# Half swaps, a broadcast and 64-bit weight loads moved to other steps of an attention loop

## The chip, the cores and the metric

One core of a Trainium2 chip runs the whole program in one launch. The metric is the device time of one execution in microseconds (us). The kernel before took 1222.17 us (median of three runs, 1221.45 to 1222.9).

## What is computed

The reference chains three parts; the change lies in the first and touches how weights of the second arrive.

```python
# attention over 16 (batch, head) pairs, seq 1152, head_dim 64; queries are averaged in pairs: 576 per head
q_pool = q.reshape(B, H, S // 2, 2, D).mean(axis=3)
attn   = softmax(q_pool @ k.T / sqrt(D))
x      = (attn @ v)  ->  (1152, 512)
# a dense layer with mish: w_in is 512 x 2048, w_out is 2048 x 512, both 64-bit floats in memory
x = mish(x @ w_in) @ w_out
# eight experts, weighted by a gate that is normalised eight times over rows and columns
out = sum_e P[:, e] * (relu(x @ w1[e]) @ w2[e])
```

## The kernel before

TensorE works on a 32-bit format that keeps fewer bits than float32 (`F32R`), so each operand is split into a high and a low part ("hi" and "lo"), and a product is the sum of two or three matmuls.

**Attention in steps.** Two heads make a pair, and there are 8 pairs. A pair has 1152 pooled queries, nine tiles of 128 (`QTL` = 9): tiles 0 to 3 belong to the first head, 5 to 8 to the second, tile 4 (`MID`) holds 64 queries of each. One step of the loop at L715 handles one tile: step `g` is pair `p` and tile `t` by `divmod(g, 9)`; the document writes t0 to t8 for the step within a pair. There are 72 steps, then three that drain. In step g the engines' instructions are put out in this order:

- what was left in the list `first` by the step before (L722 to L725);
- `scores(g)` (L468): 6 matmuls (12 at t4) into `psS`, and on VectorE the negated row maximum into `e`;
- `prep` (L691): on GpSimd (POOL), splits of the next pair's q, k and v. The last of each splitting operation also starts the next load on POOL's queue (`load_kv` L343, `load_q` L350);
- the first entry of `pre`, the list made by `turn` (L699): transposes of k (`trans_k` L405) or q (`trans_q` L452);
- `transposes(g - 3)` (L546): nine transposes of the exponentials `er` into `psT`, evacuated by ScalarE (`eth`) and VectorE (`etl`);
- `hand_over(g - 1)` (L499): one DMA on the queue of SyncE (SP) copies the exponentials of the step before from `e` to `er`, 576 KB. `er` has two buffers, so this DMA waits until `transposes(g - 3)` have read theirs; `transposes(g - 1)` in step g + 2 need it landed;
- up to 9 matmuls of attention times values (`psA`), the rest of `pre`, and `exps(g)` on ScalarE;
- at t1, `turn_sums` (L510): a transpose of the row sums, a copy to `rt`. It leaves `out` in `first`; `out` (L519, at t2) sends the sums to a row in DRAM and leaves `back`; `back` (L523, at t3) reads them back broadcast over partitions into `rx` with three DMAs. `rx` is used by `split_x` (L603) on POOL after the pair's last `psA`;
- at last `run_all` (L114), which gives out what the queues "pool", "act", "dve" and "dma" hold for this step.

**Swaps.** A transposed q tile holds [hi; lo] over the 128 partitions, and its second copy has to hold [lo; hi]. `swap` (L447) makes that copy by two DMAs on SP's queue, of 64 partitions each. `trans_q(p, u)` transposes tiles 0 to 3 (u = 0), 5 to 8 (u = 1) or tile 4 (u = 2, into `qz`), and leaves its swap in `first`. The table `TURN` (L640) puts u = 0 at t6 of the pair before, u = 2 at t0 and u = 1 at t1. At t6 `turn` lists `trans_k(p + 1, 0, 1)` first and `trans_q(p + 1, 0)` second, so the second one follows after the step's `psA` matmuls. Pair 0 takes its queries another way, without swaps.

**64-bit weights.** `load_w` plans the conversion of 64-bit weights to F32R parts: `plan64` (L136) gives a DMA of 512 KB into `raw` (three buffers, L101), then shifts, sign and sum on POOL, VectorE and ScalarE, each with a due step. Six such blocks (`busy=True`, L625 and L626) are converted during attention, with first due steps 16, 25, 34, 43, 52 and 60, and `stage` = 2, so that L178 makes their DMAs due at 11.2, 20.2, 29.2, 38.2, 47.2 and 55.2: they go out at the end of steps 12, 21, 30, 39 and 48 (all t3) and 56 (t2).

So the order of SP's queue within a pair is: t1 the swap of `qz`, `hand_over`; t2 the swap of u = 1, `out`, `hand_over`; t3 `back`, `hand_over`, the weight load; t4 to t6 `hand_over`; t7 the swap of u = 0, `hand_over`; t8 and t0 `hand_over`. SP takes them strictly in this order, as do the other engines with theirs.

```python
            waiting = first + loads          # L722
            first[:], loads[:] = [], []
            for f in waiting:
                f()
            at(ts[0] - 2.4 * stage, "dma", dma)      # L178
            first.append(lambda: swap(t))            # L464
                first.append(back)                   # L521
```

Of the kernel before, what the change touches and what calls it, by code (L numbers as in the profile page):

```python
# [23 lines left out]
def pool_attention_mish_sinkhorn_kernel(  # L24
# [22 lines left out]
    NPAIR = B * H // 2  # L47
# [56 lines left out]
    def at(t, eng, f):  # L104
        queue[eng].append((t, f))
# [12 lines left out]
    def load_w(which, i, times, stage, late="pool", parts=1, busy=False):  # L118
# [11 lines left out]
        def hi(heng, c, x):  # L130
            split_hi(heng, dest()[0][:, c, :], x)

        def lo(c, x):
            split_lo(nc.vector if late == "dve" else nc.gpsimd, dest()[1][:, c, :], x, dest()[0][:, c, :])

        def plan64(u, t):  # L136
            box = {}

            def dma():
                raw = wraw.tile([P, 2 * GF], F32, tag="raw", name=f"raw{which}_{i}_{u}")  # L140
                nc.sync.dma_start(out=raw.bitcast(I64), in_=src[:, u, :])
                w = raw.rearrange("p (n two) -> p n two", two=2)
                box["l"], box["h"] = w[:, :, 0], w[:, :, 1]

            def scale(x):
                if x and busy:
                    nc.gpsimd.tensor_scalar(box["h"], box["h"], 2.0 ** -112, 0.0, op0=ALU.mult, op1=ALU.add)
                elif x:  # L150
                    nc.scalar.activation(box["h"], box["h"], AF.Copy, scale=2.0 ** -112)
                else:
                    nc.scalar.activation(box["l"].bitcast(I32), box["l"].bitcast(U32), AF.Copy, scale=2.0 ** -29)

            def shift(cs=slice(0, GF)):
                if "t" not in box:
                    box["t"] = wpools["t"].tile([P, GF], U32, tag="wt", name=f"wt{which}_{i}_{u}")
                h = box["h"][:, cs].bitcast(U32)
                if busy:
                    nc.vector.scalar_tensor_tensor(  # L160
                        out=box["t"][:, cs], in0=h, scalar=3, in1=mask.to_broadcast(list(h.shape)),
                        op0=ALU.logical_shift_left, op1=ALU.bitwise_and)
                else:
                    nc.vector.tensor_scalar(
                        box["t"][:, cs], h, 3, 0x7FFFFFF8, op0=ALU.logical_shift_left, op1=ALU.bitwise_and)

            def sign(cs=slice(0, GF)):
                t = box["t"][:, cs]
                nc.vector.scalar_tensor_tensor(  # L169
                    out=t, in0=box["h"][:, cs].bitcast(U32), scalar=0x80000000, in1=t,  # L170
                    op0=ALU.bitwise_and, op1=ALU.bitwise_or)

            def join():
                t = box["t"].bitcast(I32)
                nc.gpsimd.tensor_tensor(out=t, in0=t, in1=box["l"].bitcast(I32), op=ALU.add)  # L175

            ts = t if isinstance(t, tuple) else [t + j * stage for j in range(5)]
            at(ts[0] - 2.4 * stage, "dma", dma)  # L178
            at(ts[0], "pool" if busy else "act", lambda: scale(1))
            at(ts[0] + parts - 1, "act", lambda: scale(0))  # L180
            for j in range(parts):
                cs = slice(j * GF // parts, (j + 1) * GF // parts)
                at(ts[1] + 2 * j, "dve", lambda cs=cs: shift(cs))
                at(ts[1] + 2 * j + parts - 1, "dve", lambda cs=cs: sign(cs))
            at(ts[2], "pool", join)
            if busy and late == "pool":
                at(ts[3], "pool", lambda: hi(nc.gpsimd, u, box["t"].bitcast(F32)))
            else:
                at(ts[3], "act", lambda: hi(nc.scalar, u, box["t"].bitcast(F32)))
            at(ts[4], late, lambda: lo(u, box["t"].bitcast(F32)))  # L190
# [21 lines left out]
        if i < NG1:  # L212
            for u, t in enumerate(times):
                if t:
                    plan64(u, t)
        else:
            for u in range(2):
                plan32(u, times[2 * u:2 * u + 2])
# [79 lines left out]
    with ExitStack() as actx:  # L298
# [31 lines left out]
        for i in range(2):  # L330
            t = z_p.tile([P, 2, 2, P], F32R, name=f"qz{i}")
# [2 lines left out]

        raws, kst, vst, kT, qst, qT = {}, {}, {}, {}, {}, {}
        loader = nc.sync
        loads, first = [], []

        def heads(p):
            b, hp = divmod(p, HPB)  # L340
# [64 lines left out]
        def trans_k(p, j, c3):  # L405
            if c3 == 0:
                kT[p, j] = kt_p.tile([P, S], F32R, tag="kT", name=f"kT{p}_{j}")
            ps = ps_t.tile([P, 4, P], F32R, tag="t", name=f"psk{p}_{j}_{c3}")
            for i in range(3):
                nc.tensor.transpose(ps[:, i, :], kst[p, j][:, 3 * c3 + i].rearrange("p a d -> p (a d)"), identr)  # L410
            nc.scalar.activation(
                kT[p, j][:, c3 * TH:(c3 + 1) * TH],
                ps[:, 0:3, :].bitcast(F32).rearrange("p a d -> p (a d)"), AF.Copy)
# [5 lines left out]
        def q_tile(p, x):  # L419
            u, i = divmod(x, MID)  # L420
            if (p, u) not in qT:
                qT[p, u] = qt_p.tile([P, 2, MID, P], F32R, tag="qT", name=f"qT{p}_{u}", bufs=2)
            return qT[p, u], i

        def middle(p, ps, n):

            z = qz[p % 2]
            for j in range(2):
                nc.scalar.activation(
                    z[:, 0:n, j, j * D:(j + 1) * D], ps[:, 0:n, j * D:(j + 1) * D].bitcast(F32), AF.Copy)  # L430
# [16 lines left out]
        def swap(t):  # L447

            for a, b in ((0, D), (D, 0)):
                nc.sync.dma_start(out=t[a:a + D, 1].bitcast(F32), in_=t[b:b + D, 0].bitcast(F32))  # L450

        def trans_q(p, u):  # L452
            ps = ps_t.tile([P, 4, P], F32R, tag="t", name=f"psq{p}_{u}")
            n = min(MID, QTL - MID * u)
            for i in range(n):
                nc.tensor.transpose(  # L456
                    ps[:, i, :], qst[p][:, MID * u + i, 0:2, :].rearrange("p a d -> p (a d)"), identr)
            if u == 2:
                middle(p, ps, 1)
                t = qz[p % 2]  # L460
            else:
                t, _ = q_tile(p, MID * u)
                nc.scalar.activation(t[:, 0], ps[:, 0:n].bitcast(F32), AF.Copy)
            first.append(lambda: swap(t))  # L464

        scS, eS, erS, rsS, rxS = {}, {}, {}, {}, {}

# [42 lines left out]
        def turn_sums(p):  # L510

            ps = ps_t.tile([P, 4, P], F32, tag="t", name=f"psr{p}")
            nc.tensor.transpose(ps[0:QTL, 0, :], rsS.pop(p), ident)
            rt = rx_p.tile([QTL, P], F32, tag="rt", name=f"rt{p}")
            nc.vector.tensor_copy(rt, ps[0:QTL, 0, :])
            row = row_p.tile([QTL, P], F32, tag="row", name=f"row{p}")
            rx = rxS[p] = rx_p.tile([P, SQ], F32, tag="rx", name=f"rx{p}")

            def out():  # L519
                nc.sync.dma_start(out=row, in_=rt)  # L520
                first.append(back)  # L521

            def back():  # L523
                flat = row.rearrange("t p -> (t p)")
                for j, x, a, n in ((0, 0, 0, SQ), (1, 0, SQ + D, SQ - D), (1, SQ - D, SQ, D)):
                    nc.sync.dma_start(
                        out=rx[j * D:(j + 1) * D, x:x + n], in_=flat[a:a + n].unsqueeze(0).to_broadcast([D, n]))

            first.append(out)
# [169 lines left out]
        def turn(p, t):  # L699
            fs = []  # L700
            for j in range(2):
                pp = p + (j == 0)
                if pp < NPAIR:
                    fs += [
                        lambda pp=pp, j=j, c=c: trans_k(pp, j, c)
                        for c in range(3) if TURN["k10" if p == 0 and j == 1 else f"k{j}"][c] == t]
            for u in range(3):
                pp = p + (u == 0)
                if p == 0 and TURN["q0"][u] == t:
                    fs.append(lambda u=u: trans_q0(u + 2))  # L710
                if 0 < pp < NPAIR and TURN["q"][u] == t:
                    fs.append(lambda pp=pp, u=u: trans_q(pp, u))
            return fs

        for g in range(T0 + EARLY):  # L715
            p, t = divmod(g, QTL)
            if g == 1:
                bctx.close()
                ps_t = pool("ps_t", 4, space=PSUM)
                ps_a = pool("ps_a", 1, space=PSUM)  # L720
            pre = turn(p, t) if g < NQ else []
            waiting = first + loads  # L722
            first[:], loads[:] = [], []
            for f in waiting:
                f()  # L725
            if g < LAG:
# [607 lines left out]
```

## Time and profile before

| | |
|---|---|
| median of three runs | 1222.17 us |
| the profiled execution: its own time | 1223.26 us |
| the profiled execution: span from first to last instruction | 1221.5 us |
| TensorE (PE) matmuls, busy | 1203.7 us, 99% of the span |
| TensorE weight loads (PEld), busy | 1110.4 us, 91% |
| VectorE (DVE), ScalarE (ACT), POOL | 70%, 48%, 54% |
| attention | about the first 270 us |

The profile is of one execution. Busy time of PE is modelled and includes overlap between matmuls. A row of the timeline gives the start, the length, engine, line, operation, what is written and read, and in brackets how long the engine sat idle before it and what ended that. For a DMA the trace gives its issue on the queue and the time from there to its landing. The landing share of the 16 DMA engines (DMA share) is given by stretches.

### The profile page before, as it was taken

To read this page: it belongs to the slowest core of one execution; us is meant where nothing else is said; L and a number is where in the kernel's file an instruction comes from. 1 tells how busy PE (TensorE), PEld (TensorE's weight loads), DVE (VectorE), ACT (ScalarE), POOL (GpSimd) and SP (SyncE) were. 2 spreads that over 40 slices of the span, in tenths; PEclk is the share of its full clock that TensorE was granted. 3 is DMA by queue.
4 is the path that set the end of the run, shared out by engine and by line. 5 is a ranking of instruction groups with operands and counts; after the bars stand their busy time and mean duration, and the time that the engine had idled before them with its cause. 6 is when DMAs were issued, how large, how long until landed. Compare 5 with 4: busy or idle time off the path is not lost.

```text
span 1221.5 us, 19362 instructions
## 1 busy us (share of the span) xinstructions
PE 1203.7 (99%) x6840; PEld 1110.4 (91%) x6840; DVE 855.8 (70%) x1598; ACT 592.1 (48%) x1354; POOL 654.0 (54%) x752
## 2 busy tenths in 40 slices
PE   8899999999999999999999999999999999999998
PEld 8899999999999999898888889999888889999887
DVE  7899999876444333787866677766866777866865
ACT  7888889877544443543332233333333233333331
POOL 7667777415444331485755566555555565555551
PEclk9999999999999999999999999999999999999999
DMA  6787787653223210011111111111011111111112
GB/s 202 265 281 263 272 264 255 232 179 120 88 71 98 74 31 30 1 52 53 32 38 45 52 48 49 52 52 52 23 40 52 53 44 52 53 52 38 37 39 78
DMA packets 51985, 116.39 MB, mean 95 GB/s; under 512 B 7977, under 2 KB 22897, under 8 KB 51889
## 3 DMA queue, kind: packets, MB, share of 16 engines
q1 hardware_dynamic: 48400, 103.36, 25.9%
q0 software_dynamic: 3488, 11.80, 3.3%
q8 instruction: 54, 0.88, 0.3%
q14 instruction: 43, 0.34, 0.1%
HBM read 66.86 MB, written 2.40 MB: 57 GB/s over the span
## 4 chain that ended last, share of the span: by engine, by line
PE 90%; DVE 5%; DMA 4%; ACT 1%; issue 1%; POOL 0%; POOLq 0%; ACTq 0%
PE po L1237 30%; PE c L1067 26%; PE ph L231 10%; PE po L806 8%; PE psS L478 4%; PE psA L581 4%; DMA er<-e 4%; PE psT L560 3%; DVE e L483 2%; DVE etl L566 1%; PE psk L410 1%; PE psw L646 0%; ACT eth L563 0%; PE pg L861 0%; PE psq L456 0%
## 5 line engine op out<-in xcount | busy, mean ns | idle before, releaser
L83 POOL TENSOR_TENSOR wslotsl<-s,wslotsh 128x256 fp32r<-128x256 f32 x180 | 132.0, 743 | 237.1 <-ACT wslotsh L76 237.1
L1245 DVE SCALAR_TENSOR_TENSOR oacc<-po,Pm,oacc 128x512 f32<-128x512 f32 (+1 forms) x217 | 161.1, 746 | 102.2 <-PE po L1237 95.8
L1237 PE MATMUL po<-wdbl,hhall 128*128 128x512 f32 (+1 forms) x543 | 214.4, 395 | 0.0
L1237 PE MATMUL po<-wdbh,hlall 128*128 128x512 f32 (+1 forms) x543 | 214.1, 394 | 0.0
L1237 PE MATMUL po<-wdbh,hhall 128*128 128x512 f32 (+1 forms) x543 | 214.0, 394 | 0.0
L1084 ACT ACTIVATE t<-c 128x384 f32<-128x384 f32 x80 | 39.3, 491 | 246.2 <-PE c L1067 246.2
L1104 ACT ACTIVATE hhall<-c 128x384 fp32r<-128x384 f32 x180 | 88.6, 492 | 127.4 <-DVE c L1100 124.7
L1237 PEld LDWEIGHTS po<-wdbh,hhall 128*128 128x128 f32 x543 | 102.1, 188 | 24.3
L1237 PEld LDWEIGHTS po<-wdbl,hhall 128*128 128x128 f32 x543 | 102.1, 188 | 23.3
L1237 PEld LDWEIGHTS po<-wdbh,hlall 128*128 128x128 f32 x543 | 102.1, 188 | 23.2
L83 POOL TENSOR_TENSOR wslotsl<-rawu,wslotsh 128x256 fp32r<-128x256 f32 x120 | 90.9, 772 | 49.8 <-ACT wslotsh L76 49.8
L483 DVE TENSOR_SCALAR_CACHE_REDUCE e<-psS 128x1152 f32<-128x1152 f32 x72 | 97.3, 1352 | 22.0 <-PE psS L478 11.7
L566 DVE TENSOR_TENSOR etl<-psT,eth 128x384 fp32r<-128x384 f32 (+1 forms) x240 | 108.0, 507 | 4.8 <-ACT eth L563 4.2
L563 ACT ACTIVATE eth<-psT 128x384 fp32r<-128x384 f32 (+1 forms) x240 | 92.8, 477 | 15.6 <-PE psT L560 15.2
L1105 DVE SCALAR_TENSOR_TENSOR hlall<-c,hhall 128x384 fp32r<-128x384 f32 x180 | 98.7, 548 | 2.1
L1067 PE MATMUL c<-x2l,wslotsh 128*128 128x384 f32 x280 | 94.3, 337 | 0.0
L1067 PE MATMUL c<-x2h,wslotsl 128*128 128x384 f32 x280 | 94.1, 336 | 0.0
L1067 PE MATMUL c<-x2h,wslotsh 128*128 128x384 f32 x280 | 93.8, 335 | 0.0
L497 ACT ACTIVATE e<-e,nm 128x1152 f32<-128x1152 f32 x70 | 89.3, 1276 | 0.1
L175 POOL TENSOR_TENSOR wt<-wt,raw 128x512 int32<-128x512 int32 x32 | 42.4, 1325 | 84.0 <-DVE wt L169 59.8
L478 PE MATMUL psS<-kT,qT 128*128 128x384 f32 x384 | 81.9, 348 | 2.8 <-DVE e L483 2.7
L76 ACT ACTIVATE wslotsh<-s 128x256 fp32r<-128x256 f32 x180 | 72.0, 411 | 24.3 <-DVE s L1033 24.3
(365 smaller groups left out, 3117.2 us busy)
## 6 DMA issues: line engine op xcount, KB each, us to landing
er<-e SPq DMA_DIRECT2D x70, 576.0 KB, 4.1
rawd<-in_moe_w_dram SPq DMA_DIRECT2D x60, 256.0 KB, 2.7
rawu<-in_moe_w_dram SPq DMA_DIRECT2D x30, 384.0 KB, 3.3
raw<-in_moe_w_in_dram SPq DMA_DIRECT2D x16, 512.0 KB, 4.3
raw<-in_moe_w_out_dram SPq DMA_DIRECT2D x16, 512.0 KB, 3.7
vraw<-in_v_dram POOLq DMA_DIRECT2D x15, 288.0 KB, 4.7
kraw<-in_k_dram POOLq DMA_DIRECT2D x13, 288.0 KB, 4.6
qT<-qT SPq DMA_DIRECT2D x28, 128.0 KB, 3.1
```

What stands on the lines that cost most here:

```text
L83: eng.tensor_tensor(out=lo, in0=src, in1=hi.bitcast(F32), op=ALU.subtract)
L231: nc.tensor.matmul(ps[:, 0:TH], lhsT=a, rhs=b, start=(n == 0), stop=(n == len(ops) - 1))
L478: nc.tensor.matmul(ps[:, kb, 0:TH], lhsT=a, rhs=kt[:, kb * TH:(kb + 1) * TH], start=(n == 0), stop=(n == len(ops) - 1))
L483: nc.vector.tensor_scalar(sc, ps[:, :, 0:TH], -1.0, None, op0=ALU.mult, op1=ALU.min, accum_out=nm)
L497: nc.scalar.activation(e, sc, AF.Exp, bias=nm, scale=-1.0, accum_out=rsS[p][:, t:t + 1])
L563: nc.scalar.activation(eh[:, cs, o:o + b - a], ps[:, 0:3, a:b], AF.Copy)
L566: nc.vector.tensor_tensor(out=el[:, cs, o:o + b - a], in0=ps[:, 0:3, a:b], in1=eh[:, cs, o:o + b - a].bitcast(F32), op=ALU.subtract)
L806: nc.tensor.matmul(ps[:, 0:TH], lhsT=a, rhs=b, start=(n == 0), stop=(n == len(ops) - 1))
L1067: nc.tensor.matmul(cb[c], lhsT=a_, rhs=b_, start=FIRST[n] and m == 0, stop=LAST[n] and m == len(ops) - 1, skip_group_check=True)
L1105: los.append(lambda: nc.vector.scalar_tensor_tensor(out=lo, in0=b, scalar=0.0, in1=hi.bitcast(F32), op0=ALU.max, op1=ALU.subtract))
L1237: nc.tensor.matmul(ps[:, 0:w], lhsT=a, rhs=b[:, cs], start=(n == 0), stop=(n == len(ops) - 1))
L1245: nc.vector.scalar_tensor_tensor(out=oa, in0=ps[:, 0:w], scalar=gate, in1=oa, op0=ALU.mult, op1=ALU.add)
```

## The change

Five edits, all in how the steps are put out; no instruction is added or removed.

- The DMAs of the six 64-bit blocks of the attention stage become due 10 steps before their conversion, not 4.8: at steps 6, 15, 24, 33 and 42 (all t6) and 50 (t5).
- The swaps of u = 1 and u = 2 go out one step later: at t3 and t2. That of u = 0 stays at t7.
- `back` goes out one step later, at t4, except for the last pair.
- At t6 `trans_q(p + 1, 0)` is listed ahead of `trans_k(p + 1, 0, 1)`, so it runs ahead of the step's `transposes`, and the transposes of k follow after `psA`.
- `loads`, a list that is always empty, goes.

```diff
-            at(ts[0] - 2.4 * stage, "dma", dma)
+            at(ts[0] - (10 if busy else 2.4 * stage), "dma", dma)
...
-        loads, first = [], []
+        first = []
...
-            first.append(lambda: swap(t))
+            first.append((lambda: swap(t)) if u == 0 else lambda: first.append(lambda: swap(t)))
...
-                first.append(back)
+                first.append(back if p == NPAIR - 1 else lambda: first.append(back))
...
-                    fs.append(lambda pp=pp, u=u: trans_q(pp, u))
+                    fs.insert(0 if u == 0 else len(fs), lambda pp=pp, u=u: trans_q(pp, u))
...
-            waiting = first + loads
-            first[:], loads[:] = [], []
+            waiting, first[:] = list(first), []
```

SP's order within a pair becomes: t1 `hand_over`; t2 the swap of `qz`, `out`, `hand_over`; t3 the swap of u = 1, `hand_over`; t4 `back`, `hand_over`; t5 `hand_over`; t6 `hand_over`, the weight load; t7 the swap of u = 0, `hand_over`; t8 and t0 `hand_over`.

## Rows read from the trace of the kernel before

**Rows 1.** The page: busy us, share of the span and instructions of each engine.

```profile
PE 1203.7 (99%) x6840; PEld 1110.4 (91%) x6840; DVE 855.8 (70%) x1598; ACT 592.1 (48%) x1354; POOL 654.0 (54%) x752
```

**Rows 2.** Waits of PE: who waited for whom, us in total, times, longest.

```profile
PE psT L560 <- DMA er<-e: 7.6, 8, 2.0
```

**Rows 3.** Timeline of PE: five of the eight waits for `er`.

```profile
22.68 0.93 PE L560 MATMUL psT<-identr,er 128*128 128x128 f32 x9 [0.53 <-DMA er<-e]
...
36.62 0.94 PE L560 MATMUL psT<-identr,er 128*128 128x128 f32 x9 [1.03 <-DMA er<-e]
...
59.67 0.93 PE L560 MATMUL psT<-identr,er 128*128 128x128 f32 x9 [1.96 <-DMA er<-e]
...
120.35 0.94 PE L560 MATMUL psT<-identr,er 128*128 128x128 f32 x9 [0.60 <-DMA er<-e]
...
216.85 0.93 PE L560 MATMUL psT<-identr,er 128*128 128x128 f32 x9 [1.67 <-DMA er<-e]
```

**Rows 4.** Stretches: busy us by engine, granted clock, DMA share, GB/s.

```profile
154.00:162.00 8.00, 7.89 (x66) 7.53 (x65) 6.93 (x16) 7.64 (x20) 7.61 (x8) 1.00 0.67 242
...
205.00:217.00 12.00, 10.33 (x80) 10.00 (x79) 9.63 (x21) 8.76 (x19) 4.31 (x5) 1.00 0.98 308
```

**Rows 5.** Timeline of SP's DMA issues, pairs 1 (48 to 52 us) and 6 (206 to 211).

```profile
48.20 0.49 SPq L503 DMA_DIRECT2D er<-e  x1
48.73 0.60 SPq L141 DMA_DIRECT2D raw<-in_moe_w_in_dram  x1
52.17 8.96 SPq L503 DMA_DIRECT2D er<-e  x3
...
206.82 0.60 SPq L141 DMA_DIRECT2D raw<-in_moe_w_out_dram  x1
208.98 1.75 SPq L526 DMA_DIRECT2D rx<-row  x3
210.83 10.65 SPq L503 DMA_DIRECT2D er<-e  x4
```

**Rows 6.** DMA issues at 52.1, 210.8 and 124.4 us: KB, us to landing.

```profile
er<-e SPq DMA_DIRECT2D x1, 576.0 KB, 7.4
qraw<-in_q_dram POOLq DMA_DIRECT2D x1, 512.0 KB, 7.3
...
er<-e SPq DMA_DIRECT2D x1, 576.0 KB, 5.9
...
er<-e SPq DMA_DIRECT2D x1, 576.0 KB, 3.0
```

**Rows 7.** Timeline of SP's DMA issues, pair 0, t7 and t8.

```profile
28.98 1.12 SPq L450 DMA_DIRECT2D qT<-qT  x2
30.38 7.72 SPq L503 DMA_DIRECT2D er<-e  x3
```

**Rows 8.** Stretches of 1 us, columns as in rows 4.

```profile
32.00:33.00 1.00, 1.00 (x12) 1.00 (x11) 1.00 (x4) 1.00 (x3) 0.00 (x0) 1.00 0.45 101
...
157.00:158.00 1.00, 1.00 (x9) 0.96 (x8) 0.72 (x3) 1.00 (x2) 1.00 (x3) 1.00 0.98 410
```

**Rows 9.** Timeline of POOL: the last split of pair 1's queries; the first use of `rx` in pair 6.

```profile
21.12 1.42 POOL L83 TENSOR_TENSOR qst<-qraw,qst 128x576 fp32r<-128x576 f32 x1
...
215.74 1.39 POOL L607 TENSOR_TENSOR xs<-xs,rx 128x576 f32<-128x576 f32 x1 [7.31 <-DMA rx<-row]
```

**Rows 10.** Timeline of SP's DMA issues, pair 4, t5 to t8.

```profile
152.61 3.68 SPq L503 DMA_DIRECT2D er<-e  x2
157.37 1.13 SPq L450 DMA_DIRECT2D qT<-qT  x2
159.38 3.18 SPq L503 DMA_DIRECT2D er<-e  x2
```

**Rows 11.** Timeline of PE: `psT` at t0 after pair 4's t8.

```profile
164.35 0.93 PE L560 MATMUL psT<-identr,er 128*128 128x128 f32 x9
```

**Rows 12.** The page, DMA issues: count, KB each, median us to landing.

```profile
qT<-qT SPq DMA_DIRECT2D x28, 128.0 KB, 3.1
```

## The prediction

> **What bounds the kernel now.** I read the page first: TensorE's matmuls are busy for 1203.7 of 1221.5 us [rows 1]. So a change of order can give back at most its idle time, 17.8 us. The waits come next: the largest one is that of the transposes `psT` for the copy `er`, 7.6 us in eight places [rows 2]; nothing else of that size is in reach of this change. The timeline shows where the eight lie: two in pair 0 (0.53 us at 22.68 and 1.03 at 36.62), the other six between 59 and 217 us at t4 to t6 of pairs 1, 2, 3, 5 and 6, from 1.96 us down to 0.41 (three of them are in [rows 3]). 7.6 − 0.53 − 1.03 leaves 6.0 us for these six.
>
> Each is one transfer that landed late. `er` is handed over in step g, when `psT` of that step has freed a buffer, and read two steps on. Unhindered it lands in 3.0 us; the one behind the wait at 59.67 took 7.4, that behind 216.85 took 5.9 [rows 6]. SP's timeline shows what went before them: the 512 KB weight block goes out at 48.73, between the copies at 48.20 and 52.17; in pair 6 the block goes out at 206.82, the three broadcast DMAs at 208.98 occupy SP for 1.75 us, and the copy follows only at 210.83 [rows 5]. By the stretches the DMA engines are full there (share 0.98 over 205 to 217), while around t5 to t7 of pair 4 the share is 0.67 [rows 4]. So the six waits are work crowded into t1 to t4, and three of the five edits take work out of just these steps.
>
> **The weight block, from t3 to t6.** The same six DMAs, 0.60 us each on SP, come about six steps earlier. Their buffers are three: the block due at step 33 takes that of the first one, whose last reader is due at step 23 (16 + 7), and so on with ten steps between, so no DMA waits for a buffer. What they leave: 512 KB less ahead of the copy at t4. At the 410 GB/s that the engines reach when they move copies alone [rows 8] that is 1.28 us of all 16 engines. What they meet at t6: in pair 4 the copies go out at about 155.8 (the second issue of the row that begins at 152.61) and 159.38, and the latter is read at 164.35 [rows 10, 11], so 5.0 us are allowed. Between them now come the block (1.28 us of transfer), the swap (256 KB: at least 0.64 us at 410 GB/s, at most the 1.4 us of a copy, since a half of it lands in 3.1 us [rows 12] where a copy took 3.0; I take 1.1, as its smaller pieces lie nearer the upper end) and the first copy itself (576 KB, 1.4 us): 3.8 us of transfer in 3.6 us of time. A backlog of 0.2 us on a landing of 3.0 makes 3.2, well inside 5.0. SP needs 0.48 + 0.60 + 1.13 = 2.2 us of issue in those 3.6, so the second copy isn't issued late either. Cost there: nothing; the cover is 1.8 us of slack, and if it went, `psT` at t0 would wait.
>
> In pair 0 it is not free. Step 6 lies at about 25 to 28 us, while the first loads of q, k and v are under way. The copy issued at 30.38 [rows 7] took 6.1 us or so to be read at 36.62, and PE already waits 1.03 us for it [rows 3]. Now a block goes ahead of it. The upper bound is the block's whole 1.28 us. The lower is that less the time in which the engines idled just then, 0.55 us of the stretch from 32 to 33 [rows 8]: 0.7. I take +1.0, nearer the middle since only some of the engines have the gap.
>
> **The broadcast, a step later.** `back` waits for the row in DRAM, and its three issues hold SP 1.75 us ahead of the copy [rows 5]. A step later the row has long landed and the copy of t3 goes first, by up to 1.9 us (210.83 − 208.98) earlier. At t4 the three issues come behind a copy and have a step of 3 us and more to themselves. Queued behind them is only the next copy. The reader of `rx` is `split_x` on POOL; in pair 6 it waited for `rx` until 215.74 [rows 9]. There the issue moves from 208.98 to just behind the copy and the weight block is gone, so it lands no later. PE doesn't read its result at these steps. Nothing, with bounds of 0.2 us to either side, the scatter of the smaller waits.
>
> **The swaps of u = 1 and u = 2, a step later.** They no longer go ahead of the copies of t1 and t2 but right behind the one before or after it; their source is then ready, so SP waits for nothing. A swap lands in 3.1 us in the median [rows 12], about one step; `scores` needs it at t4 and t5, still two steps on. Nothing; if that failed PE would wait in `psS`.
>
> **The first queries, first at t6.** The same matmuls change places within the step. They need the split of q from POOL, done by 22.5 us in pair 0 [rows 9], where step 6 begins at about 25; later pairs have more room. The swap then goes out right behind a copy rather than ahead of the next (28.98 before 30.38 [rows 7]). Nothing by itself. Dropping `loads` costs nothing, for the list is always empty.
>
> **The sum.** Of the 6.0 us I take 5.6 as won: the waits of 0.41 to 0.60 go whole, since an `er` of these steps gains 1.28 us from the block or the time of the broadcast's issues; of the wait of 1.96 us I leave 0.4, because POOL's load of q (7.3 us to landing [rows 6]) crowds the same copy and doesn't move. Plus 1.0 in pair 0: −4.6 us. Outside attention nothing changes; PE then simply runs on earlier. The profiled execution took 1223.26 us: 1218.7. The median of the runs shown stands 1.1 us below it, so 1217.6.
>
> One rule of the Trainium skill speaks against part of this. The page "DMA: Bandwidth & Descriptors", section "Queues, rings and completion order", says that on each DMA engine the descriptors of a ring are taken in order, and that rows of different issuers take turns. By that the block in pair 0 costs the copy behind it its whole transfer, and the sum would be 0.3 us worse, −4.3.
>
> **Rivals.**
>
> *POOL's loads are the cause.* The copy that took 7.4 us was issued together with POOL's load of q, which took 7.3 [rows 6], and this load stays where it is. If it alone holds the copies back, the waits of pairs 1, 2 and 5 and the first of pair 3 remain, and only those at 216.85 (1.67) and 120.35 (0.60) go [rows 3]: −2.3 + 1.0 = −1.3, 1220.9 us. Against it: the wait at 216.85, the second longest, has no load of q near it. Chance 0.2.
>
> *The crowd moves along (slower).* If a copy at t7 of pairs 1 to 4, with block and swap ahead of it, lands as late as that of pair 1 did beside its block (7.4 us [rows 6]), each of four pairs waits 7.4 − 5.0 = 2.4 us at t0: +9.6. With 1.3 in pair 0 and the old 6.0 gone that is +4.9, 1227.1 us. It decides once that copy takes over 5.0 us. Against it stands the DMA share of 0.67 there, with no other load of more than 288 KB [rows 4]. Chance 0.06.
>
> *Everything goes.* If the earlier swap of pair 0 outweighs the block, its 1.03 us go as well: −7.0, 1215.2 us. Chance 0.12.
>
> **How the numbers follow.** The forecast has the other 0.62. Its own bounds are −3.3 (1.0 us left over in pair 1, 0.3 more in pair 5, 1.3 in pair 0, against 6.0: −3.4) and −5.4 (nothing left over, 0.6 in pair 0), that is 1216.8 to 1218.8; the runs shown scatter by 0.75 us to either side, so 1216.0 to 1219.6. The range reaches to most of the last rival below and of the first above: 1215.0 to 1221.2. A measurement of this kernel can tell about 0.2%, 2.4 us, from no change, so faster means under 1219.7: all but a little of the forecast (0.58), the last rival (0.12) and a little of the first (0.04): 0.74. Same: 0.21. Slower: 0.05.
>
> **What would show it.** Right: the waits of `psT` for `er` fall from 7.6 us to about 3, those left are the two in pair 0 (the one at about 36 us now 2 us) and perhaps one near 58; the copies at t2 to t4 land in under 5.5 us; the DMA share at t6 and t7 rises and the copies there land in under 4. The span falls by what the waits lose. Wrong: waits for `er` at t8 or t0 (the crowd moved), or waits left at t4 to t6 beside loads of q (POOL's loads), or PE waiting in `psS` for a swap, or `psS` for VectorE in place of `er`.

## The result, and the profile after

The changed kernel took 1235.84 us in the median of four runs (1234.7 to 1237.64). Beside it the kernel before took 1221.81 (1220.49 to 1222.9): a ratio of 1.0117, 95% interval 1.0099 to 1.0134. It is slower by 14 us where 4.6 us less were forecast, and lies outside the range. The profiled execution took 1236.56 us with a span of 1234.5, 13.0 more than before.

Three lines of the page after, for [rows 1] and [rows 12]:

```profile
span 1234.5 us, 19371 instructions
...
PE 1211.0 (98%) x6840; PEld 1113.3 (90%) x6840; DVE 864.8 (70%) x1598; ACT 592.4 (48%) x1354; POOL 652.9 (53%) x752
...
qT<-qT SPq DMA_DIRECT2D x28, 128.0 KB, 4.5
```

The waits of PE after (us in total, times, longest), for [rows 2]:

```profile
PE psS L478 <- DVE e L483: 4.5, 6, 1.5
PE psS L478 <- DMA qT<-qT: 4.3, 4, 2.3
PE psT L560 <- DMA er<-e: 4.0, 6, 1.6
PE psk L898 <- DVE csum L892: 1.9, 2, 1.6
```

The wait that the change was read against did shrink, from 7.6 to 4.0 us. In its place stand a wait for the swap `qT`, of which there was none before, and more waiting for VectorE (2.7 us before). Together they don't make 13 us. The rest is seen when the start of each step's `scores` is compared in the two timelines. By the start of its last step attention is 10.3 us late, which to some tenths is made of:

- won: 6.1 us, in the steps where PE had waited for `er` (1.8 of them for the wait near 217 us of [rows 3]);
- lost at t0 of pairs 1 to 5, where `scores` needs the swap of u = 0: 2.95 + 1.64 + 0.40 + 0.66 + 1.41 = 7.1 us. In it are 4.3 us of waits for the swap, 1.0 for the copies `er` of t7, which go out behind the swap, and 1.5 of a lower clock in pair 1; the 1.03 that PE waited there before is taken off;
- lost in waits for `er` at t6 of pair 2 and at t5 and t6 of pair 4: 1.6 us. The copies read there went out two steps before, at t3 and t4, that of t4 directly behind `back`;
- lost in t1 to t3 of pairs 3 and 5, with no large wait for a DMA: 4.4 + 3.7 = 8.1 us.

The remaining 2.7 us lie near 565 us, at the gate, where PE waited 1.6 us for `csum` (0.6 before), and then ran 3.4 us at a granted clock of 0.50, which loses 1.7. Other kernels of this study whose times were within 0.1% of before (g2 and g4 below) have the same longer wait, so I count it to the scatter between executions.

**The swap.** SP's DMA issues after, in pairs 0 and 4 (start, us held); [rows 7] and [rows 10] are the same places before:

```profile
26.81 0.58 SPq L141 DMA_DIRECT2D raw<-in_moe_w_in_dram  x1
27.49 1.50 SPq L450 DMA_DIRECT2D qT<-qT  x2
29.73 9.53 SPq L503 DMA_DIRECT2D er<-e  x3
...
132.54 0.55 SPq L141 DMA_DIRECT2D raw<-in_moe_w_in_dram  x1
133.14 1.54 SPq L450 DMA_DIRECT2D qT<-qT  x2
```

The DMA issues after from 133.0 to 134.6 us (KB, us to landing):

```profile
raw<-in_moe_w_in_dram SPq DMA_DIRECT2D x1, 512.0 KB, 5.9
qT<-qT SPq DMA_DIRECT2D x2, 128.0 KB, 5.5
```

PE's timeline after: three of the four places where `scores` waits for the swap (pairs 1, 4 and 5), and the second line, at t0 of pair 2, where `psT` waits for the copy that went out at t7:

```profile
36.10 1.11 PE L478 MATMUL psS<-kT,qT 128*128 128x384 f32 x5 [2.27 <-DMA qT<-qT]
...
72.83 0.94 PE L560 MATMUL psT<-identr,er 128*128 128x128 f32 x9 [0.76 <-DMA er<-e]
...
139.75 1.12 PE L478 MATMUL psS<-kT,qT 128*128 128x384 f32 x5 [0.36 <-DMA qT<-qT]
...
172.91 1.12 PE L478 MATMUL psS<-kT,qT 128*128 128x384 f32 x5 [1.15 <-DMA qT<-qT]
```

The block is the DMA directly ahead of the swap of u = 0, and they land close together (138.5 us, and 139.6 for the swap's second half), the swap after 5.5 us where 3.1 was the median [rows 12]. The Trainium skill's page "DMA: Bandwidth & Descriptors", section "Queues, rings and completion order", says that a ring's descriptors are taken in order; the trace agrees, with this 5.5 beside 3.1.

**The broadcast.** SP's timeline after in pair 2:

```profile
84.73 0.48 SPq L503 DMA_DIRECT2D er<-e  x1
85.31 2.57 SPq L526 DMA_DIRECT2D rx<-row  x3
```

The first use of that `rx`, on POOL, before and then after (the wait after is put down to VectorE, which had long been done, so it was `rx`, the larger part of which took 7.5 us to land):

```profile
87.77 1.42 POOL L607 TENSOR_TENSOR xs<-xs,rx 128x576 f32<-128x576 f32 x1 [5.06 <-DVE xs L598]
```

```profile
93.75 1.41 POOL L607 TENSOR_TENSOR xs<-xs,rx 128x576 f32<-128x576 f32 x1 [7.43 <-DVE etl L566]
```

POOL's work is 6.0 us later there, PE's only 3.2. What that does shows 10 us on. VectorE, POOL and PE before, t1 of pair 3 (start, us, engine, line, operation):

```profile
102.93 1.27 PE L478 MATMUL psS<-kT,qT 128*128 128x384 f32 x6
...
102.00 0.72 DVE L160 SCALAR_TENSOR_TENSOR wt<-raw,mask 128x256 uint32<-128x256 uint32 x1
...
104.44 0.15 DVE L507 TENSOR_TENSOR rs<-rs,eps 128x9 f32<-128x9 f32 x1
...
105.22 1.44 POOL L83 TENSOR_TENSOR kst<-kraw,kst 128x576 fp32r<-128x576 f32 x1
...
106.52 1.29 PE L478 MATMUL psS<-kT,qT 128*128 128x384 f32 x6
```

The same step after:

```profile
107.36 1.26 PE L478 MATMUL psS<-kT,qT 128*128 128x384 f32 x6
...
106.32 0.68 POOL L390 TENSOR_SCALAR qraw<-qraw 128x576 f32<-128x576 f32 x1
106.96 1.42 POOL L83 TENSOR_TENSOR vst<-vraw,vst 128x576 fp32r<-128x576 f32 x1
...
106.44 2.23 DVE L160 SCALAR_TENSOR_TENSOR wt<-raw,mask 128x256 uint32<-128x256 uint32 x1
...
110.39 1.66 DVE L507 TENSOR_TENSOR rs<-rs,eps 128x9 f32<-128x9 f32 x1
...
110.58 1.44 POOL L83 TENSOR_TENSOR kst<-kraw,kst 128x576 fp32r<-128x576 f32 x1
...
113.61 1.32 PE L478 MATMUL psS<-kT,qT 128*128 128x384 f32 x6 [0.89 <-DVE e L483]
```

The step took 3.59 us before (102.93 to 106.52) and 6.25 after. `L507`, nine numbers a partition, took 0.15 us in a gap of POOL before; after, it ends at 112.05, just as POOL's `L83` ends (112.02). `L160` ends at 108.67, 0.29 us behind POOL's `L390` and `L83` (108.38). Behind the two on VectorE stand `etl` and `e`, for which PE waits. Over the whole kernel, VectorE's groups by form before and after (busy us, mean ns):

```profile
L160 DVE SCALAR_TENSOR_TENSOR wt<-raw,mask 128x256 uint32<-128x256 uint32 x12 | 6.2, 517 | 0.0
...
L507 DVE TENSOR_TENSOR rs<-rs,eps 128x9 f32<-128x9 f32 x8 | 1.6, 206 | 0.0
```

```profile
L160 DVE SCALAR_TENSOR_TENSOR wt<-raw,mask 128x256 uint32<-128x256 uint32 x12 | 11.6, 966 | 0.0
...
L507 DVE TENSOR_TENSOR rs<-rs,eps 128x9 f32<-128x9 f32 x8 | 4.3, 543 | 0.0
```

The Trainium skill's page "SBUF — State Buffer", section "SBUF: two separate sides", says that VectorE and GpSimd share a pair of ports under an exclusive lock, that a VectorE operation with two inputs in SBUF takes part in it against a GpSimd operation that reads SBUF, and that whichever starts second is blocked until the other's instruction is done. The traces agree: the two that stretch have both inputs in SBUF, and they end when POOL's instructions do, `L160` behind the second of two in a row.

### The profile page after: what moved, and what is told of

The parts are those of the page before. It is cut to its first block, busy times and chain, and to the rows that moved or that the text cites. A ratio compares the mean times of both kernels' runs of the same rounds, so it can differ in the third digit from the quotient of the medians.

```text
span 1234.5 us, 19371 instructions
## 1 busy us (share of the span) xinstructions
PE 1211.0 (98%) x6840; PEld 1113.3 (90%) x6840; DVE 864.8 (70%) x1598; ACT 592.4 (48%) x1354; POOL 652.9 (53%) x752
## 4 chain that ended last, share of the span: by engine, by line
PE 90%; DVE 4%; DMA 4%; ACT 1%; issue 1%; SPq 0%; POOL 0%; POOLq 0%; ACTq 0%
PE po L1236 30%; PE c L1066 25%; PE ph L231 10%; PE po L805 8%; PE psS L478 5%; PE psA L581 4%; DMA er<-e 3%; PE psT L560 3%; DVE etl L566 1%; DVE e L483 1%; PE psk L410 1%; DVE wt L160 1%; ACT eth L563 0%; DMA qT<-qT 0%; ACT e L497 0%
## 5 line engine op out<-in xcount | busy, mean ns | idle before, releaser
L83 POOL TENSOR_TENSOR wslotsl<-s,wslotsh 128x256 fp32r<-128x256 f32 x180 | 131.6, 740 | 239.9 <-ACT wslotsh L76 239.9
L83 POOL TENSOR_TENSOR wslotsl<-rawu,wslotsh 128x256 fp32r<-128x256 f32 x120 | 91.1, 773 | 50.2 <-ACT wslotsh L76 50.2
```

Of the source, the lines that this page charges most:

```text
L83: eng.tensor_tensor(out=lo, in0=src, in1=hi.bitcast(F32), op=ALU.subtract)
```

## The experiments

Each ratio is against runs of the kernel before on the same chip. The theory that grew out of the comparison: (1) the block ahead of the swap makes `scores` wait at t0; (2) the late broadcast makes POOL late, and late POOL meets VectorE's operations on SBUF. The rivals: either of the two alone, or the copies and the bandwidth.

**One part alone: the block (e1).**

```diff
-            at(ts[0] - 2.4 * stage, "dma", dma)
+            at(ts[0] - (10 if busy else 2.4 * stage), "dma", dma)
```

> Only the weight blocks go out ten steps ahead; broadcast, swaps and order as before. Theory (two costs: the block ahead of the swap of u = 0 makes psS wait at t0; the later broadcast delays POOL, whose work then falls on VectorE's): psS waits for the swap as in the changed kernel or more (4 to 8 us, the swap goes out after the transposes at the end of t6), waits for er at t4 to t6 shrink by 3 to 5, no shift on VectorE above 1.1 us; 1222 to 1228 us. Rival (the block alone does all of it, POOL's lateness too): shifts of 1.5 to 2.2 us appear and the time is 1232 to 1237.

Measured: 1224.28 us in ten runs (1223.2 to 1226.38) against 1220.26, ratio 1.0029 (1.0018 to 1.0041). Its waits of PE:

```profile
PE psS L478 <- DMA qT<-qT: 4.2, 4, 2.8
...
PE psT L560 <- DMA er<-e: 1.7, 4, 0.6
```

The copies win 5.9 us, more than I had forecast for them, the swap costs 4.2 us of waits that weren't there, and VectorE's `L160` stays at 488 ns. These alone would leave a gain. What turns it into a loss in the profiled execution is TensorE's clock. PE was busy 4.49 of the 7.4 us from 28.0 and 2.46 of the 4 from 69.0; after each its granted clock is 0.50, the lower of its two levels (1.2 GHz; columns as in [rows 4]):

```profile
35.45:42.28 6.83, 6.41 (x28) 6.14 (x29) 2.76 (x5) 1.89 (x5) 0.00 (x0) 0.50 0.50 192
73.00:76.40 3.40, 3.40 (x18) 3.40 (x18) 2.96 (x6) 1.26 (x3) 0.00 (x0) 0.50 0.58 230
```

Together 10.2 us at half speed are 5.1 us of lost work, and 4.2 + 5.1 − 5.9 = 3.4, where the span is 2.8 longer than before. The other nine executions had a mean clock of 0.997 to 0.999, this one 0.995. This is half (1) by itself, with what the clock adds to its waits.

**The broadcast alone (e2).**

```diff
-                first.append(back)
+                first.append(back if p == NPAIR - 1 else lambda: first.append(back))
```

> Only the broadcast goes out a step later. Theory: rx lands after POOL could have used it, split_x starts later in most pairs, POOL's splits then meet VectorE's shifts (some above 1.4 us, against 0.98 before); no wait for a swap; 1223 to 1231 us. Rival (the block does it): no shift above 1.1 us, 1220 to 1222.5.

Measured: 1234.32 us (1231.83 to 1238.24), ratio 1.0113 (1.0082 to 1.0144): more than expected, and nearly the whole loss of the change. PE doesn't wait for a swap here; `L160` takes 952 ns in the mean, `L507` 540. The waits for `er` stay at 7.0 us, of which 6.4 lie at t6 of pairs 1 to 3, where the copy of t4 is read, which now goes out behind `back`. POOL now waits for `rx` in five places, 48.8 us in all, where it was two and 30.0 before (the longest, 22.9 us, is the last pair's, whose broadcast wasn't moved). Two of the new ones in POOL's timeline:

```profile
57.41 1.39 POOL L607 TENSOR_TENSOR xs<-xs,rx 128x576 f32<-128x576 f32 x1 [1.71 <-DMA rx<-row]
...
126.08 1.40 POOL L607 TENSOR_TENSOR xs<-xs,rx 128x576 f32<-128x576 f32 x1 [7.81 <-DMA rx<-row]
```

**The swaps of u = 1, 2 with the order of t6 (e3), and the order alone (g4).** Both have the second edit:

```diff
-            first.append(lambda: swap(t))
+            first.append((lambda: swap(t)) if u == 0 else lambda: first.append(lambda: swap(t)))
...
-                    fs.append(lambda pp=pp, u=u: trans_q(pp, u))
+                    fs.insert(0 if u == 0 else len(fs), lambda pp=pp, u=u: trans_q(pp, u))
```

> Only the swaps of u = 1 and 2 a step later and the first queries first at t6; block and broadcast as before. Both theories: no wait of psS for a swap, waits for er down by 1 to 2 us, 1219.5 to 1221.5 us. If these edits carry a cost of their own, it shows as a time above 1223.

> Before, with the first queries first at t6 and nothing else. Both theories: within 1.5 us of before; waits for er within 1 us of 7.6. If the order alone shifts POOL against VectorE, stretched operations appear and the time is above 1223.

Measured: e3 1225.72 us in ten runs (1221.43 to 1230.56), ratio 1.0048 (1.003 to 1.0067), a miss; PE waits 8.5 us for `er`, and `L160` stays at 551 ns. g4 1219.86 (1216.65 to 1222.89), ratio 0.9993 (0.998 to 1.0006): no cost. Its waits for `er` are 4.1 us and not within 1 us of 7.6, a miss too: this figure moves by 3.5 us between traces of kernels that take the same time. The later swaps cost something as long as the broadcast is not moved with them: at t3 the swap of u = 1 and `back` then both stand ahead of `hand_over`. The trace bears that out, for 7.4 of e3's 8.5 us lie at t5, where the copy of t3 is read; the swaps without the order were not tried.

**All but one part (e4, f2).** Against the changed kernel, e4 puts the broadcast back, f2 the block:

```diff
-                first.append(back if p == NPAIR - 1 else lambda: first.append(back))
+                first.append(back)
```

```diff
-            at(ts[0] - (10 if busy else 2.4 * stage), "dma", dma)
+            at(ts[0] - 2.4 * stage, "dma", dma)
```

> The changed kernel with the broadcast back in its old step. Theory: the stretched shifts on VectorE in pairs 3 and 5 go (none above 1.1 us) and with them some 8 us; the waits of psS for the swap stay (3 to 5 us); 1225 to 1229 us. Rival (the block alone): as the changed kernel, 1233 to 1237, stretched shifts still there.

> The changed kernel with the weight blocks in their old steps. Theory: no wait of psS for a swap, rx late and VectorE's operations stretched as with the broadcast alone, waits for er at t4 to t6 as before or more; 1229 to 1236. Rival (the block alone is the cost): 1219 to 1223.

Measured: e4 1234.01 us (1230.05 to 1236.22), ratio 1.0104 (1.0075 to 1.0132); f2 1238.55 (1237.77 to 1240.87), ratio 1.0157 (1.014 to 1.0173). Both missed, on the slow side. In e4 VectorE's operations are short again (512 ns), as half (2) has it, but PE waits 8.6 us for `er` and 6.3 for the swap: t3 is crowded as in e3 (7.1 of the 8.6 lie at t5), and 10.2 us at a granted clock of 0.50 take another 5.1. In f2 the swap of u = 0 is never late, but `L160` takes 1237 ns, `er` 8.1 us of waits, and 13.7 us at the lower clock take 6.8. PE waits once for a swap, 0.9 us at t5 of pair 6, where the sixth block, at t2, is directly ahead of the swap of u = 1, now at t3. The parts don't add up: alone they cost 0.29, 1.13 and 0.48%, together 1.17%.

**The block behind the swap of u = 0 (f1).** One number of the changed kernel, so that the block falls due a step later:

```diff
-            at(ts[0] - (10 if busy else 2.4 * stage), "dma", dma)
+            at(ts[0] - (9 if busy else 2.4 * stage), "dma", dma)
```

> The changed kernel with the weight blocks nine steps ahead, so that each goes out at t7, behind the swap of u = 0 and not ahead of it. Theory (block ahead of the swap; late broadcast delays POOL): no wait of psS for a swap, the stretched operations of VectorE (above 1.4 us) stay; 5 to 8 us below the changed kernel, 1226 to 1230. Rival (all of it comes from the broadcast): the same as the changed kernel, 1233 to 1237.

Measured: 1228.44 us (1227.34 to 1230.27), ratio 1.0072 (1.0056 to 1.0088), that is 0.45% or 5.5 us better than the changed kernel by the ratios. Its waits of PE, and VectorE's groups:

```profile
PE psS L478 <- DVE e L483: 6.3, 8, 1.5
...
PE psT L560 <- DMA er<-e: 1.3, 3, 0.7
...
PE psS L478 <- DMA qT<-qT: 1.0, 1, 1.0
```

```profile
L160 DVE SCALAR_TENSOR_TENSOR wt<-raw,mask 128x256 uint32<-128x256 uint32 x12 | 13.8, 1151 | 0.0
...
L507 DVE TENSOR_TENSOR rs<-rs,eps 128x9 f32<-128x9 f32 x8 | 7.4, 921 | 0.0
```

Half (1) is nearly gone, the copies are at their best, and the granted clock is 1.00 throughout. The 1.0 us for a swap that is left lies at t0 of pair 6, and it has the same cause: the sixth block, due at step 51, still goes out at t6, directly ahead of the swap at 193.87:

```profile
193.48 0.34 SPq L141 DMA_DIRECT2D raw<-in_moe_w_out_dram  x1
```

What remains is half (2), which grew: `L160` from 966 to 1151 ns, `L507` from 543 to 921.

**POOL without the wait for `rx` (g1, g2).** g1 is the changed kernel, g2 is f1, each with this line, so that POOL's order and its work, but for 0.3 us a pair (`L607` takes 1.14 us, not 1.42), stay and the division by the row sums is left out of the output:

```diff
-                nc.gpsimd.tensor_tensor(out=xs, in0=xs, in1=rxS.pop(p), op=ALU.mult)
+                nc.gpsimd.tensor_tensor(out=xs, in0=xs, in1=xs, op=ALU.mult)
```

> The changed kernel, but split_x multiplies the tile by itself and not by rx, so that POOL waits for no broadcast (the division by the row sums is left out). All DMAs stay. Theory (the late rx holds POOL, whose work then meets VectorE's): POOL no longer waits for rx in attention, few or no operations of VectorE above 1.4 us, waits of psS for the swap stay at 3 to 5 us; 6 to 9 us below the changed kernel, 1226 to 1230. Rival (POOL's lateness comes from PE's waits for the swap): as the changed kernel, 1233 to 1237.

> The same with the weight blocks nine steps ahead, behind the swap of u = 0 (the division by the row sums is left out here too). Theory: both costs gone, waits for the swap under 1 us, VectorE's operations as before; 1216 to 1221 us. Rival (stretched operations come with the swaps or the order): 1226 to 1230, as with the broadcast's wait.

Measured: g1 1229.49 us (1226.67 to 1230.05), ratio 1.0066 (1.005 to 1.0082); g2 1220.48 in ten runs (1217.55 to 1229.93), ratio 0.9998 (0.9975 to 1.002). So the wait for `rx` is worth 0.51% (6.2 us) in the changed kernel and 0.74% (9.0 us) in f1, and with both halves taken away the loss is gone. What g1 still loses is half (1) and its clock: 2.9 us of waits for the swap and 10.2 us at a granted clock of 0.50. `L160` is back at 625 and 604 ns. The broadcast's DMAs still run in both, at the same places in SP's order; so it is the waiting of POOL for them that costs, not their traffic.

**Before, with POOL made late (h1).** No DMA is moved. POOL repeats a split of 0.67 us three times ahead of `split_x`, in pairs 0 to 6:

```diff
+                for _ in range(3 if p < NPAIR - 1 else 0):
+                    split_hi(nc.gpsimd, xh[:, hp, sl], xs)
```

> Before, all DMAs in their old steps, but POOL does the first half split of xs three times more ahead of split_x (0.68 us each, overwritten after; about 2 us), so that its later work is some 2 us late, as behind a late rx. Theory (POOL's lateness alone stretches VectorE's operations): operations above 1.4 us appear in two or more pairs, no wait for a swap; 4 to 12 us above before, 1224 to 1233. Rival (the late rx is only a sign, the crowd of DMAs costs the time): within 1.5 us of before.

Measured: 1239.07 us (1236.03 to 1240.64) against 1218.5, ratio 1.016 (1.0139 to 1.018), more than expected. VectorE's groups of h1, then its timeline near 100 us:

```profile
L160 DVE SCALAR_TENSOR_TENSOR wt<-raw,mask 128x256 uint32<-128x256 uint32 x12 | 23.6, 1967 | 0.0
...
L507 DVE TENSOR_TENSOR rs<-rs,eps 128x9 f32<-128x9 f32 x8 | 7.3, 914 | 0.0
```

```profile
98.97 1.44 POOL L388 TENSOR_TENSOR qraw<-qraw 128x576 f32<-128x576 f32 x1
99.78 3.56 DVE L160 SCALAR_TENSOR_TENSOR wt<-raw,mask 128x256 uint32<-128x256 uint32 x1
100.37 0.67 POOL L80 TENSOR_SCALAR vst<-vraw 128x576 fp32r<-128x576 f32 x1
101.02 0.67 POOL L390 TENSOR_SCALAR qraw<-qraw 128x576 f32<-128x576 f32 x1
101.65 1.40 POOL L83 TENSOR_TENSOR vst<-vraw,vst 128x576 fp32r<-128x576 f32 x1
```

`L160` starts 0.81 us after POOL's run of four and ends 0.29 after it (103.34, against 103.05), as it did at 108.67 in the changed kernel. PE waits 0.6 us for `er` and not at all for the swap, so half (2) needs no late DMA, only a POOL that is late or busier. The three splits are 2 us more of POOL's work a pair, and the trace holds 17.1 us at a granted clock of 0.50, 8.5 us of lost work; how much of the 1.6% is the work and how much the delay, this run doesn't part.

The fifteen traces together bear half (2) out. Each of the 16 pairs in which `L507` took 1.65 us or more spent 13.5 to 16.4 us in t1 to t3. Of the other 89 (pairs 1 to 7), 88 spent 10.2 to 12.9, and one 14.1 (in g3, where an `L160` of t2 took 1.51). All 52 `L160` of more than 1 us end 0.28 or 0.29 us behind the end of a POOL instruction.

**Looking for a better version (g3, f3, f4).** g3 is f1 with `split_x` one step later and a second buffer for `xs`; f3 and f4 are the kernel before with the order of t6 and the block at 8 or 9 steps instead of 4.8. The line of g3:

```diff
-                    late.append(lambda: late.append(lambda: split_x(p)) if p < NPAIR - 1 else split_x(p))
+                    late.append(lambda: late.append(lambda: late.append(lambda: split_x(p))) if p < NPAIR - 1 else split_x(p))
```

> The changed kernel with the blocks nine steps ahead, and split_x put out one step later (its tile xs in two buffers), so that POOL comes to it when rx has landed. Theory: POOL waits for rx 1 us or less each, fewer stretched operations; 1217 to 1225 us. Rival: 1226 to 1230, as without the later split_x.

> Before, with the weight blocks eight steps ahead (t8, behind the swap of u = 0) and the first queries first at t6; broadcast and the other swaps as before. Theory: no wait for a swap, no stretched operation above 1.2 us, waits for er below 3 us: 2 to 5 us below before, 1215 to 1219. Rival (any earlier block costs): slower than before.

> As the one with eight steps, but nine ahead (t7, right behind the swap of u = 0). Theory: 2 to 5 us below before, 1215 to 1219, with the swap landing in under 4 us. Rival (any earlier block costs): slower than before.

Measured, ten runs each: g3 1226.01 us (1220.97 to 1230.38), ratio 1.0038 (1.0021 to 1.0055); f3 1221.62 (1217.45 to 1228.56), ratio 1.0021 (1.0003 to 1.0038); f4 1223.85 (1217.18 to 1227.27), ratio 1.0022 (1.0001 to 1.0043). g3, just above what was expected, regains half of f1's loss: `L160` falls from 1151 to 810 ns. f3 and f4 were to be faster and are not, though the waits for `er` fall to 2.8 us in f3 and 4.8 in f4. `L160` takes 761 ns in f3, 2.9 us more in all; whether that is where the gain went was not tried. None of the thirteen beats the kernel before beyond the scatter.

## Why the prediction was wrong

**Right for the block: the copies of t2 to t4.** Waits for `er` were to fall from 7.6 to about 3 us with 5.6 us won at t4 to t6. They fell to 4.0 with 6.1 us won in the steps' starts, 5.5 of them at t4 to t6, and to 1.7 with the block alone (e1). The 4.0 proves little by itself, for g4 shows 4.1 with no block moved. The rival that POOL's loads of q hold the copies back falls with e1, where the wait of 1.96 us in pair 1 is down to 0.42. The order at t6 costs nothing, as said (g4). (Of the bounds, −3.3 is −3.4 by its own terms; nothing hangs on it.)

**Wrong: "Cost there: nothing; the cover is 1.8 us of slack".** The step weighed the block against the copy at t7 and put the swap into that sum as load, not as something that is waited for. But the first thing behind the block on SP's ring is the swap of u = 0, and `scores` reads it at t0. It lands after 5.5 us where 3.1 had been; the block's own landing is 5.9, not 1.28 us of transfer. The copy of t7 was mis-sized as well: in pair 1 it took 6.5 us (issued at 66.31, read at 72.83), not 3.2, and its 5.0 us of cover were not enough. Price: 7.1 us in five places, against 1.0 forecast for pair 0 alone; the swap is 4.3 of that, the copy of t7 1.0. The rival "the crowd moves along" had place and sign and was given 0.06; its condition was met in pair 1, but it priced the copy alone. f1, with the swap ahead of five of the six blocks, shows the step's failure apart: 5.5 us back, the clock included.

**Mis-sized: "I take +1.0" in pair 0.** Measured 2.95 us. PE waits 2.27 for the swap and 0.23 for `er`, where it waited 1.03 for `er` before: 1.5 more. The other 1.5 I put down to the clock. Stretches after (us of PE, PEld, DVE, ACT, POOL busy; granted clock, DMA share, GB/s):

```profile
32.00:36.00 4.00, 1.83 (x13) 1.52 (x11) 2.73 (x6) 2.84 (x7) 0.00 (x0) 1.00 1.05 311
38.00:39.00 1.00, 1.00 (x9) 1.00 (x8) 1.00 (x3) 0.91 (x3) 0.00 (x0) 0.56 0.15 60
40.00:41.00 1.00, 1.00 (x5) 1.00 (x5) 0.41 (x1) 0.00 (x0) 0.00 (x0) 0.50 0.95 378
```

PE had been busy 1.83 of 4 us; from 38.1 to 41.5 its granted clock is 0.50, the lower of its two levels (1.2 GHz), where it was 1.00 before. These 3.4 us at half speed are 1.7 us of lost work, 0.2 of it in the step after. The prediction priced no wait by what the clock does after it. In the trace of before no stretch of attention shows less than 1.00. In others 0.50 stands for 6.8 us (e2), 10.2 (e1, e4 and g1), 13.7 (f2) and 17.1 (h1), half of which is lost work. So the clock is a large term here, and no run parts it from the waits.

**Wrong: "PE doesn't read its result at these steps. Nothing, with bounds of 0.2 us".** True of PE, and the wrong question. What had to be named is what stands behind `split_x` on POOL: the splits of v, k and q of the next pairs, which then come at another place beside VectorE's `L160` and `L507`: ahead of pairs 3 and 5 POOL reaches `L607` 6.0 and 10.6 us later, 2.8 and 2.4 more than PE is late there. "There the issue ... lands no later" was said of pair 6 and carried to all; in pair 2 the issue moved from 80.07 to 85.31, of which PE's own lateness is 3.6. Price: 8.1 us in pairs 3 and 5 of the trace; 6.2 and 9.0 us by g1 and g2; and 1.1% where it is the only edit (e2). "Queued behind them is only the next copy" had a price too: of the 4.0 us that PE still waits for `er`, 2.6 lie at t6, where that copy is read, and 6.4 of 7.0 in e2, against 0.4 with the block alone (e1). h1 shows that lateness of POOL does it with no DMA moved.

**Wrong in part: "The swaps of u = 1 and u = 2 ... Nothing".** In the changed kernel no wait of theirs is seen; without the broadcast's move they cost 0.48% (e3), and with the block left at t2 and t3 one of them is late (f2).

**What stays open.** Why pairs 3 and 5 are hit and not 4 and 6: ahead of the former POOL reaches `L607` 0.6 to 0.7 us after the start of t6's `scores`, ahead of the latter 1.5 before it, but in f1 pairs 3 and 4 are hit with the same 1.5. Why f1 has longer stretches than the changed kernel. And why g2, f3 and f4 don't turn fewer waits for `er` into less time; f4's trace is of an execution of 1219.44 us, 4.4 below its median, so it doesn't show what the others lose.

## What to carry to other kernels

When a transfer is moved earlier, list everything behind it on the same ring with the step at which each is read; the swap, not the big copy, was the tight one here. When a wait moves onto an engine that nobody seems to wait for, ask what that engine's queue will then run beside: 2.4 to 2.8 us of delay on POOL against PE, ahead of two pairs, cost PE 8 us through VectorE operations that read two operands from SBUF. Add to the price of a wait what the granted clock does after it. And test parts in combinations, for three parts that cost 0.29, 1.13 and 0.48% alone cost 1.17% together.

## What was unexpected of the hardware

A VectorE operation on 128x9 took 0.15 us in a gap of POOL and 1.66 beside it, and one on 128x256 between 0.41 and 3.61 us. In the changed kernel and in h1 `L160` stayed held through two and four POOL instructions in a row, until POOL's run of them was over, not only through the one that it met; it ended 0.29 us behind the last one each time. And a wait of 2.3 us was followed by 3.4 us at half the clock, 1.7 us more.
